# v of three pairs loaded through GpSimd's casting queue, and a new written-out order of work

## The chip, the core and the metric

The kernel runs on one NeuronCore of a Trainium2 chip. The metric is the device time of one execution in microseconds, lower is better. Each kernel is executed several times, and the median is compared. One further execution is recorded by the hardware profiler; all lines of the profile come from that one.

The engines of the core take their instructions from a queue each, in order: TensorE (PE, with its weight loads PEld), VectorE (DVE), ScalarE (ACT), GpSimd (POOL) and SyncE (SP), which here only issues DMAs.

## What is computed

Two stages, one after the other. The first is a gated linear attention over 4 batches, 8 heads, 768 steps and head dimension 48; the second is a two-layer network on the 3072 rows of 384 that the first gives.

```python
def _attn_ref(q, k, v, f_logit):
    f = 1.0 / (1.0 + np.exp(-f_logit))
    state = np.zeros((B, H, D, D))
    for t in range(S):
        state = f[:, :, t, :, None] * state + np.einsum('bhd,bhe->bhde', k[:, :, t], v[:, :, t])
        y[:, :, t] = np.einsum('bhd,bhde->bhe', q[:, :, t], state)

def _moe_ref(x, w_in, w_out):        # x: (3072, 384), w_in: (384, 2048)
    h = x @ w_in
    g = 0.5 * (h + np.sqrt(h * h + 4.0))
    return g @ w_out
```

## The kernel before

The 3072 rows are cut into 12 pairs of 128-step chunks (256 steps, all 8 heads; three pairs make a batch). For each pair `p` the function `describe` makes pieces of work, named by a short code, the pair and a part. Pair 0 is handled in two halves of four heads (`.0` and `.1`) up to its keys and queries; the others in one. The pieces, with the lines that the profile gives for them:

- `lf lq lk lv` (L174): loads of the logits, q, k and v by SyncE, 384 KB each (192 KB for a half of pair 0).
- `ex` (L181), `ut`, `tt`, `ln` (L248), `hi` (L258, or a cast), `lo` (L266): exp of the logits, its sum with one, the product over two steps, its logarithm and the split of that into two fp16 parts. `cu` (L283, L289) sums the logarithms along the steps by matmuls with a triangle; `ep`, `ea` (L312) are exponentials of the sums, from pair 3 on `c1` (L302) adds for the second.
- `qu ku qm km` (L142): q and k scaled by the decays. `tp` and `te` (L390 and a copy) transpose them on TensorE for pairs 0 to 3; `tx` (L373) does it by a DMA for pairs 4 to 11.
- `vc`: v cast to fp16 (L137 on ScalarE, L139 on the others).
- `sc` (L414) scores, `pm` (L429) masks them, `kv` (L442) key times value, `ia` (L452) or `sp` (L468) adds the old state, `sa` and `sb` scale it, `yt` (L492) and `yn` (L501) give y, `yc` copies y out of PSUM. `ge gs gb` are small factors of the state.
- `xp` (L525) and `xe`, or a DMA `xx` (L516) from pair 4 on, transpose y into x.
- `m1` (L541, eight pieces a pair) is x times w_in, `sq` (L550) the square, `rt` (L556) the square root, `gt` (L566) the sum, `m2` (L578, two times four pieces) g times w_out, `ev` copies the result out of PSUM, `st` (L598) stores it.
- `wi0` to `wi3` and `wo0` to `wo3`: the weights, cast to fp16 on the way by DMAs that GpSimd issues (L148, L153), 384 KB of fp16 each. `m1` pieces 0 and 1 need `wi0`, 2 and 3 `wi1`, and so on.

Nothing in the kernel decides the order at run time or at build time: the string `ORDER` names each piece once, with the engine that runs it (after the colon) and the PSUM banks that it fills (after the @). The kernel goes through it word by word, so the order of the words that go to one engine is the order of that engine's queue; the framework only adds the waits. `TABLE:e` and `TABLE:s` load ScalarE's tables for exp and log, and for the square root. `DEPTH` gives how many buffers a tile has, eight PSUM banks are handed out in the words. A piece that needs something late holds up all that stands behind it on its engine. Where a word begins with `wm`, the loop would issue matmuls on constants whose result nobody reads; `ORDER` has no such word.

Of the kernel before, what the change touches and what calls it, by code (L numbers as in the profile page):

```python
# [40 lines left out]
lv2.0:S gt0.0:D yt1:T@23 ku2.0:P sq0.4:A yn1.0:T sa1:D m1.0.3:T@7 rt0.2:A yc1.0:D ia1.1:T m1.0.2:T@4 gt0.1:D sq0.3:A lo3.0:P
yn1.1:T sb1:D xp1.0:T@0 sq0.2:A km2.0:D wo1:P rt0.1:A cu3.0:T@2 lk3.0:S m1.0.6:T@6 qu2.0:P yc1.1:D TABLE:e ln4.0:A c13.0:D
xp1.1:T@3 lq4.0:S qm2.0:P xe1.1:D xe1.0:D m1.0.7:T@3 gt0.5:D ex5.0:A m1.1.1:T@0 gt0.2:D lq3.0:S ea3.0:A vc2.0:P gt0.4:D
tp2.0:T@14 ge3:A sq0.7:A wo0:P ut5.0:D m1.1.3:T@5 sq1.1:A te2.1.0:D tt5.0:P sq0.6:A te2.0.0:D ep3.0:A wo2:P ln5.0:A lk4.0:S
gt0.3:D sc2.0:T@41 TABLE:s rt0.3:A hi4.0:P pm2.01:D kv2:T@27 wo3:P ia2.0:T pm2.00:D m1.1.0:T@1 lo4.0:P sa2:D m1.1.2:T@4
lf6.0:S sq1.3:A gt0.7:D ku3.0:P ia2.1:T sc2.1:T@27 sq1.2:A gt0.6:D m1.1.5:T@3 rt1.1:A pm2.10:D m1.1.4:T@6 hi5.0:P pm2.11:D
sq1.0:A m2.0.00:T@2 km3.0:P gt1.3:D rt1.0:A m2.0.01:T gt1.2:D yt2:T@57 sq1.4:A yn2.0:T gt1.0:D yn2.1:T qu4.0:P sq1.5:A
m1.1.7:T@4 yc2.1:D rt1.2:A m1.1.6:T@1 lo5.0:P gt1.1:D lf7.0:S cu4.0:T@7 qu3.0:D sq1.6:A gs3:P m2.0.10:T@0 sq1.7:A yc2.0:D
qm3.0:P m2.0.11:T rt1.3:A gt1.4:D xp2.0:T@5 m2.0.02:T lk5.0:S gt1.5:D TABLE:e ep4.0:A cu5.0:T@6 gt1.7:D ku4.0:P xp2.1:T@3
m2.0.12:T xe2.0:D lv3.0:S c15.0:D tp3.0:T@45 ex6.0:A c14.0:D m2.0.03:T km4.0:P xe2.1:D ep5.0:A lf8.0:S te3.0.0:D m2.0.13:T  # L50
ge5:A ex7.0:A te3.1.0:D m1.2.2:T@6 ge4:A lv4.0:S ev0.0:A ut7.0:D sc3.1:T@73 sc3.0:T@45 ea5.0:A m2.1.10:T@2 ut6.0:D tt7.0:P
ev0.1:A lq5.0:S gt1.6:D m2.1.11:T ea4.0:A sq2.2:A tt6.0:D m2.1.12:T qm4.0:P vc3.0:A m1.2.0:T@0 pm3.10:D m2.1.13:T ln6.0:A
pm3.00:D sq2.0:A m1.2.3:T@1 pm3.11:D ln7.0:A gb4:P kv3:T@47 tx4.0:S ku5.0:D hi6.0:P sq2.3:A m2.1.00:T@3 TABLE:s rt2.1:A sa3:D
m2.1.01:T st0.01.0:S km5.0:P sp3.1:D tx4.1:S m1.2.1:T@4 pm3.01:D m2.1.02:T ev1.1:D lv5.0:S yt3:T@57 sq2.1:A lo6.0:D qu5.0:P
lq6.0:S yn3.1:T rt2.0:A gt2.3:D m1.2.5:T@2 gt2.2:D m2.1.03:T qm5.0:P yc3.1:A m1.2.4:T@1 gt2.1:D yc3.0:A lk6.0:S ev1.0:A
sc4.1:T@56 gt2.0:D sq2.4:A sc4.0:T@47 m1.2.6:T@3 pm4.11:D sb3:P sq2.5:A lf9.0:S xp3.1:T@0 pm4.00:D rt2.2:A m1.2.7:T@6 vc4.0:P
pm4.01:D m2.2.10:T@4 sq2.7:A st1.01.1:S st0.01.1:S gs4:P gt2.4:D hi7.0:P m2.2.11:T sq2.6:A qu6.0:P gt2.5:D xp3.0:T@7 cu6.0:T@1
rt2.3:A tx5.0:S pm4.10:D m2.2.12:T lo7.0:P TABLE:e ex8.0:A xe3.1:D yt4:T@25 gt2.7:D ku6.0:P yn4.0:T tx5.1:S m2.2.00:T@0
xe3.0:D gt2.6:D kv4:T@67 lq8.0:S c16.0:D ex9.0:A cu7.0:T@3 vc5.0:P sp4.0:D m2.2.01:T ea6.0:A ut8.0:D ep7.0:A m2.2.13:T lk7.0:S
sa4:D tt8.0:P ge6:A yc4.0:A m1.3.0:T@6 c17.0:D ep6.0:A yn4.1:T ev2.1:D m2.2.02:T ea7.0:A gb5:P ut9.0:D gs5:P ln8.0:A  # L60
m1.3.1:T@4 ge7:A yc4.1:D kv5:T@12 sq3.0:A tt9.0:P sp4.1:D sc5.1:T@23 xx4:S sq3.1:A m2.2.03:T pm5.11:D sb4:P ln9.0:A sc5.0:T@57
pm5.10:D TABLE:s rt3.0:A lv8.0:S m1.3.3:T@3 km6.0:P pm5.01:D lq7.0:S m1.3.5:T@2 sp5.0:D m1.3.4:T@7 lv6.0:S ev2.0:D m1.3.2:T@1
sa5:P pm5.00:D sq3.4:A sq3.5:A gt3.1:D yt5:T@05 hi9.0:P st1.01.0:S rt3.2:A yn5.0:T qm6.0:P yn5.1:T m1.4.1:T@4 yc5.0:D sq3.3:A
gt3.5:D m1.3.7:T@0 sq3.2:A gt3.0:D m1.3.6:T@2 lo9.0:P tx6.0:S rt3.1:A gt3.4:D m1.4.3:T@6 vc6.0:P yc5.1:D sq3.7:A m1.4.4:T@7
lv7.0:S gt3.3:D sq3.6:A qu7.0:P m2.3.10:T@5 tx6.1:S rt3.3:A gt3.2:D m1.4.0:T@3 hi8.0:P gs6:D m2.3.11:T lv9.0:S ku7.0:P sq4.1:A
gt3.6:D m2.3.12:T sq4.0:A gt3.7:D kv6:T@12 rt4.0:A lf10.0:S m1.4.2:T@0 sa6:D vc8.0:P sq4.4:A gt4.0:D m2.3.13:T km7.0:P sq4.3:A
m2.3.00:T@1 sp6.1:D xx5:S sq4.2:A gt4.1:D m1.4.6:T@2 rt4.1:A ev3.1:D m1.4.7:T@3 qu8.0:P lk8.0:S sc6.1:T@45 sq4.6:A gt4.3:D
m2.3.01:T gb7:P sq4.7:A pm6.10:D vc7.0:P m1.4.5:T@6 rt4.3:A lf11.0:S pm6.11:D lo8.0:P m2.3.02:T gt4.2:D sq4.5:A sc6.0:T@45
st2.01.0:S st2.01.1:S qm7.0:P m2.3.03:T rt4.2:A gt4.6:D cu8.0:T@0 pm6.00:D TABLE:e ex10.0:A cu9.0:T@2 gt4.7:D m1.5.3:T@4 sb6:P
tx7.0:S gt4.5:D m2.4.10:T@3 ku8.0:P gt4.4:D m2.4.00:T@6 tx7.1:S ge9:A ge8:A ev3.0:D ep9.0:A m2.4.11:T c18.0:D ex11.0:A lq9.0:S  # L70
m2.4.01:T ut10.0:D gs7:P ea8.0:A m2.4.12:T ut11.0:D ep8.0:A lk9.0:S m1.5.2:T@1 sq5.3:A pm6.01:D tt11.0:P m2.4.13:T sq5.2:A
c19.0:D tt10.0:P yt6:T@05 ev4.1:D ea9.0:A lv10.0:S kv7:T@27 yc6.0:D ln11.0:A yn6.1:T gb8:P m2.4.02:T sp7.0:D ln10.0:A TABLE:s
rt5.1:A yc6.1:D sc7.0:T@03 sa7:P m2.4.03:T pm7.00:D xx6:S qm8.0:P m1.5.1:T@2 sp7.1:D m1.5.0:T@0 ev4.0:D st3.01.0:S sq5.1:A
st3.01.1:S gt5.3:D m1.5.4:T@5 st4.01.1:S sq5.0:A qu9.0:P gt5.2:D m1.5.5:T@6 lq11.0:S rt5.0:A sc7.1:T@47 pm7.01:D hi11.0:P
m1.5.7:T@1 sb7:P sq5.5:A gt5.0:D m1.5.6:T@3 sq5.4:A gt5.1:D hi10.0:P m1.6.2:T@0 rt5.2:A pm7.11:D lo11.0:P m2.5.10:T@2 gs8:D
sq5.7:A m2.5.11:T km8.0:P gt5.4:D sq5.6:A m1.6.0:T@7 gt5.5:D rt5.3:A m1.6.3:T@5 pm7.10:D m2.5.12:T gs9:P sq6.2:A tx8.1:S
gt5.6:D ku9.0:P kv8:T@46 sq6.3:A yt7:T@36 sp8.0:D rt6.1:A tx8.0:S yn7.0:T yn7.1:T gt5.7:D m1.6.1:T@4 qm9.0:P sq6.0:A gt6.3:D
m1.6.5:T@1 lk11.0:S sq6.1:A gt6.2:D m2.5.13:T lk10.0:S rt6.0:A yc7.1:D m1.6.4:T@0 km9.0:P ev5.1:A cu11.0:T@5 gt6.1:D sq6.4:A
m2.5.00:T@2 gt6.0:D yc7.0:A sc8.1:T@46 c111.0:D lo10.0:P sq6.5:A xx7:S sc8.0:T@37 m2.5.01:T pm8.11:D rt6.2:A ku11.0:P
m2.5.02:T pm8.10:D tx9.1:S cu10.0:T@6 pm8.00:D m2.5.03:T gt6.4:D TABLE:e ep10.0:A lv11.0:S vc9.0:P m1.6.7:T@3 pm8.01:D  # L80
st4.01.0:S ep11.0:A m1.6.6:T@0 sa8:P gt6.5:D ge11:A ea11.0:A yt8:T@74 c110.0:D sq6.7:A qu11.0:P kv9:T@15 tx9.0:S yn8.0:T
ge10:A ea10.0:A sa9:D yn8.1:T m1.7.6:T@6 sq6.6:A yc8.1:D m1.7.2:T@1 TABLE:s rt6.3:A sp9.1:D lq10.0:S m2.6.00:T@4 vc11.0:P
yc8.0:D gb10:D m1.7.1:T@5 xx8:S ku10.0:P m1.7.3:T@7 sq7.2:A gt6.7:D m2.6.01:T sq7.3:A gt6.6:D m2.6.02:T rt7.1:A ev5.0:D
# [43 lines left out]
def describe(nc, W, ctx_tiles, aps):  # L127
# [28 lines left out]
    for p in range(NP):  # L156
# [9 lines left out]
        for x, (h0, h1) in enumerate(parts):  # L166
            hs = slice(h0, h1)
            nh = h1 - h0
            for s in "fqkv":
                def load(e, bk, s=s, x=x, hs=hs, p=p):  # L170
                    if (s, p) not in T:
                        T[s, p] = sb(s, p, [128, 8, 2, 48], FP32)
# [556 lines left out]
```

## Time and profile before

| | |
|---|---|
| time, median of 11 runs | 197.24 us (193.91 to 199.5) |
| profiled execution | 195.81 us, span 193.6 us |
| TensorE matmul | 171.9 us busy (89%) |
| VectorE, ScalarE, GpSimd | 152.1, 153.5, 117.9 us busy (79%, 79%, 61%) |
| DMA | 32.87 MB, 170 GB/s over the span |
| read, written in HBM | 25.17 MB, 4.72 MB |

The span runs from the first to the last instruction; the time is a little longer. Busy shares are averages over stages: in the first 28 us the matmuls wait for inputs to be prepared, later they follow one another. A line of the timeline gives start and duration in us, engine, line of the kernel, operation, written and read tiles, size, count, and in brackets how long the engine stood idle ahead of it and what it waited for. In the table by stretches each engine has its busy time and in brackets its number of instructions; then come the clock that TensorE was granted (1.00 is full), the mean busy share of the DMA engines, and GB/s.

### The profile page before, as it was taken

How to read it: one execution, taken by the hardware profiler on the slowest of the kernel's cores; microseconds unless marked ns; L12 is line 12 of the kernel's file. 1: busy time of each engine (PE TensorE's matmuls, PEld its weight loads, DVE VectorE, ACT ScalarE, POOL GpSimd, SP SyncE). 2: the span in 40 equal slices, each digit the busy share in tenths (PEclk: the TensorE clock that was granted, in tenths of full speed). 3: DMA queues.
4: the chain of work that ended last, by engine and by line, in shares of the span. 5: the costliest groups of instructions: out<-in, count | busy, mean ns of one | idle time of the engine just before them, and what ended most of it. 6: DMA issues, size and time to landing. Idle time of an engine off the chain costs nothing.

```text
span 193.6 us, 5596 instructions
## 1 busy us (share of the span) xinstructions
PE 171.9 (89%) x2287; PEld 124.3 (64%) x2287; DVE 152.1 (79%) x280; ACT 153.5 (79%) x246; POOL 117.9 (61%) x146
## 2 busy tenths in 40 slices
PE   0348994899999999899999999999989999999990
PEld 0235772667666766687667776877657688767650
DVE  5797898898898999887999988867769787536640
ACT  4685899599989998899979989987756599896600
POOL 5159559898989779939989996859950100000000
PEclk9999999699999999999999999999999999999998
DMA  5999999999987999999999989991687234000623
GB/s 148 271 261 241 249 218 232 253 236 208 261 205 125 217 254 130 272 217 211 212 243 207 244 148 206 187 197 51 54 151 138 43 85 83 3 0 3 163 73 90
DMA packets 80506, 32.87 MB, mean 170 GB/s; under 512 B 73825, under 2 KB 80481, under 8 KB 80481
## 3 DMA queue, kind: packets, MB, share of 16 engines
q1 hardware_dynamic: 76768, 29.37, 74.3%
q0 software_dynamic: 3712, 3.15, 10.1%
q8 instruction: 18, 0.29, 0.6%
q14 instruction: 8, 0.06, 0.1%
HBM read 25.17 MB, written 4.72 MB: 154 GB/s over the span
## 4 chain that ended last, share of the span: by engine, by line
PE 69%; DMA 18%; DVE 4%; issue 2%; POOL 2%; ACT 2%; SPq 1%; DVEq 0%; ACTq 0%
PE ps L578 30%; PE ps L541 27%; DMA xT<-y 6%; DMA win<-in_moe_w_in_dram 4%; DMA f<-in_f_logit_dram 3%; PE ps L414 3%; DMA k<-in_k_dram 2%; DMA qkT<-qk 2%; PE ps L492 2%; PE ps L442 2%; DVE qk L142 2%; PE ps L501 2%; PE ps L283 1%; POOL k L142 1%; PE ps L390 1%
## 5 line engine op out<-in xcount | busy, mean ns | idle before, releaser
L566 DVE SCALAR_TENSOR_TENSOR g<-ps,r 128x512 f16<-128x512 f32 x96 | 62.3, 682 | 17.6 <-ACT r L556 17.6
L541 PE MATMUL ps<-xT,win 128*128 128x256 f16 x576 | 73.6, 275 | 2.1 <-DMA xT<-y 0.8
L578 PE MATMUL ps<-wout,g 128*128 128x384 f16 x384 | 71.1, 326 | 0.0
L550 ACT ACTIVATE hsq<-ps 128x512 f16<-128x512 f32 x96 | 54.0, 592 | 15.7 <-PE ps L541 15.0
L541 PEld LDWEIGHTS <-win 128*128 128x128 f16 x576 | 55.2, 99 | 14.0 <-issue 1.5
L556 ACT ACTIVATE r<-hsq 128x1024 f16<-128x1024 f16 x48 | 50.6, 1057 | 1.2
L578 PEld LDWEIGHTS <-g 128*128 128x128 f16 x384 | 36.1, 98 | 19.5
L429 DVE TENSOR_TENSOR pm<-ps,mask 128x512 f16<-128x512 f32 x48 | 30.8, 681 | 3.0 <-PE ps L414 3.0
L142 POOL TENSOR_TENSOR qk<-q,ea 128x384 f16<-128x384 f32 x22 | 22.2, 1032 | 1.3 <-DVE q L142 0.8
L142 POOL TENSOR_TENSOR k<-k,UT 128x768 f32<-128x768 f32 x9 | 16.3, 1815 | 3.6 <-DMA k<-in_k_dram 1.9
L142 POOL TENSOR_TENSOR qk<-k,ep 128x384 f16<-128x384 f32 x18 | 17.6, 998 | 0.1
L283 PE MATMUL ps<-hl,tri 128*128 128x384 f16 (+1 forms) x34 | 9.3, 376 | 8.8 <-ACT hl L258 6.6
L181 ACT ACTIVATE f<-f 128x768 f32<-128x768 f32 (+1 forms) x13 | 10.3, 791 | 4.7 <-DMA f<-in_f_logit_dram 4.4
L139 POOL CAST v<-v 128x768 f16<-128x768 f32 (+1 forms) x11 | 9.1, 823 | 5.7 <-DMA v<-in_v_dram 5.7
L142 POOL TENSOR_TENSOR UT<-UT 128x384 f32<-128x384 f32 (+1 forms) x9 | 9.1, 1013 | 4.2 <-DVE UT L231 4.2
L142 POOL TENSOR_TENSOR q<-q,UT 128x384 f32<-128x384 f32 x9 | 9.0, 1001 | 3.8 <-DMA q<-in_q_dram 3.8
L266 POOL TENSOR_TENSOR hl<-s,hl 128x384 f16<-128x384 f32 (+1 forms) x11 | 10.4, 950 | 0.8 <-ACT hl L258 0.7
L137 ACT COPY os<-ps 128x384 f32<-128x384 f32 x9 | 4.3, 480 | 8.1 <-PE ps L578 5.0
L414 PE MATMUL ps<-qkT 48*64 48x128 f16 x384 | 9.5, 228 | 1.3 <-ACT qkT L137 0.6
L414 PEld LDWEIGHTS <-qkT 48*64 48x64 f16 x384 | 6.6, 110 | 5.4 <-issue 3.2
L139 DVE CAST y<-ps 128x384 f16<-128x384 f32 x17 | 9.2, 548 | 0.9 <-PE ps L501 0.9
L139 DVE COPY os<-ps 128x384 f32<-128x384 f32 x15 | 8.2, 546 | 2.1 <-PE ps L578 2.1
(71 smaller groups left out, 185.9 us busy)
## 6 DMA issues: line engine op xcount, KB each, us to landing
f<-in_f_logit_dram SPq DMA_DIRECT2D x11, 384.0 KB, 6.0
k<-in_k_dram SPq DMA_DIRECT2D x11, 384.0 KB, 5.6
q<-in_q_dram SPq DMA_DIRECT2D x11, 384.0 KB, 6.2
v<-in_v_dram SPq DMA_DIRECT2D x11, 384.0 KB, 5.8
out_dram<-os SPq DMA_DIRECT2D x22, 192.0 KB, 3.2
win<-in_moe_w_in_dram POOLq DMA_DIRECT2D x4, 384.0 KB, 8.1
wout<-in_moe_w_out_dram POOLq DMA_DIRECT2D x4, 384.0 KB, 8.2
f<-in_f_logit_dram SPq DMA_DIRECT2D x2, 192.0 KB, 3.0
```

Of the source, the lines that this page charges most:

```text
L139: eng(e).tensor_copy(out=o, in_=i)
L142: eng(e).tensor_tensor(out=o, in0=a, in1=b, op=ALU.mult)
L181: nc.scalar.activation(out=t, in_=t, func=AF.Exp, scale=-1.0)
L266: eng(e).tensor_tensor(out=hl[:, 1, hs, 0:D], in0=T["s", p][:, hs], in1=hl[:, 0, hs, 0:D], op=ALU.subtract)
L283: nc.tensor.matmul(out=T["cum", p, m][:, h0 * D:h1 * D], lhsT=tri[:, m], rhs=t[:, hs, 0:D], start=(r == 0), stop=(r == len(terms) - 1), sk ...
L414: nc.tensor.matmul(out=T["sc", p, i, h][64 * cc:64 * cc + 64, j, :], lhsT=t[r, 1, j, i, :], rhs=t[r, 0, j], start=True, stop=True)
L429: eng(e).tensor_tensor(out=T["pm", p, i, h], in0=T["pc", p, i, h] if key in PMACT else T["sc", p, i, h], in1=K["mask"][:, i].unsqueeze(1). ...
L541: nc.tensor.matmul(out=T["h", p, m][:, a], lhsT=K["win"][m // 2][:, j, m % 2 * 256 + a * 128:m % 2 * 256 + a * 128 + 128], rhs=T["xT", p][ ...
L550: nc.scalar.activation(out=T["hsq", p, r][:, a], in_=T["h", p, m].rearrange("p a c t -> p (a c t)"), func=AF.Square, scale=1.0)
L556: nc.scalar.activation(out=T["r16", p, r], in_=T["hsq", p, r], func=AF.Sqrt, scale=0.25, bias=1.0)
L566: nc.vector.scalar_tensor_tensor(out=T["g", p][:, 2 * m:2 * m + 2, :].rearrange("p a t -> p (a t)"), in0=T["h", p, m].rearrange("p a c t - ...
L578: nc.tensor.matmul(out=T["o", p, cc], lhsT=T["g", p][:, jn, cc * 128:(cc + 1) * 128], rhs=K["wout"][jn // 4][:, jn % 4, :], start=(jn == 0 ...
```

## The change

Four things are edited.

1. For pairs 1, 2 and 3 (`VDMA`) there is no load `lv` by SyncE and no cast `vc`. A new piece `vd` on GpSimd loads v straight from HBM into the fp16 tile and casts on the way.
2. `ORDER` is another one throughout: pieces stand elsewhere in the queues, some on another engine, with other PSUM banks. The set of pieces is the same but for `vd`.
3. The stores of the last pair may be issued by ScalarE; the second to last store, `st11.1.0`, is.
4. The branch for `wm` words is gone.

```diff
+VDMA = [1, 2, 3]
...
-            for s in "fqkv":
+            for s in ("fqk" if p in VDMA else "fqkv"):
...
+            if p in VDMA:
+                def vd(e, bk, x=x, hs=hs, p=p):
+                    if ("v16", p) not in T:
+                        T["v16", p] = sb("v16", p, [128, 8, 2, 48], FP16)
+                    bb, t0 = divmod(p * 256, 768)
+                    nc.gpsimd.dma_start(out=T["v16", p][:, hs].rearrange("p h i d -> p h (i d)"),
+                                        in_=v[bb][hs, t0:t0 + 256, :].rearrange("h (p i) d -> p h (i d)", i=2))
...
-                W.add(f"st{p}.{''.join(map(str, cs))}.{i}", "SP" if p in SPLIT_OUT else "S", st, ...
+                W.add(f"st{p}.{''.join(map(str, cs))}.{i}", "SPA" if p in SPLIT_OUT else "S", st, ...
...
-            if name.startswith("wm"):
-                t = ps(banks, [128, 128], FP32)
-                for n in range(int(name[2:])):
-                    nc.tensor.matmul(out=t, lhsT=ident, rhs=ident, start=True, stop=True)
-                continue
```

The queues of GpSimd and TensorE in the first third, by their words (before, then after; ScalarE and VectorE change in the same way):

```
GpSimd before: tt0.1 lo0.1 gs0 lo1.0 wi0 wi2 lo2.0 vc0.0 qm1.0 gb1 wi1 tt3.0 wi3 gs1 vc1.0 tt4.0 gs2 gb2
               hi3.0 ku2.0 lo3.0 wo1 qu2.0 qm2.0 vc2.0 wo0 tt5.0 wo2 hi4.0 wo3 lo4.0 ku3.0
GpSimd after:  lo0.0 qu0.1 lo1.0 wi0 wi2 vd1.0 vc0.1 gs0 qm1.0 wi1 wi3 tt3.0 gb1 tt4.0 hi3.0 lo3.0 gs1 gs2
               gb2 ku2.0 vd2.0 wo0 qu2.0 qm2.0 wo1 wo2 tt5.0 hi4.0 lo4.0 hi5.0 ku3.0
TensorE before: kv0 yt0 yn0.1 ia0.1 xp0.0 xp0.1 tp1.0 m1.0.1 m1.0.0 sc1.0 sc1.1 m1.0.4 m1.0.5 kv1 ia1.0 yt1
               yn1.0 m1.0.3 ia1.1 m1.0.2 yn1.1 xp1.0 cu3.0 m1.0.6 xp1.1 m1.0.7 m1.1.1 tp2.0 m1.1.3 sc2.0 kv2
TensorE after: kv0 yt0 yn0.1 ia0.1 xp0.0 xp0.1 tp1.0 m1.0.0 m1.0.1 sc1.1 sc1.0 m1.0.5 kv1 ia1.0 m1.0.4 yt1
               yn1.0 ia1.1 m1.0.3 yn1.1 m1.0.2 xp1.0 xp1.1 cu3.0 m1.0.6 m1.0.7 tp2.0 m1.1.2 kv2 ia2.0 sc2.0
```

The end of the order, where only the last store differs in kind:

```diff
-m2.11.13:T st11.0.0:S st11.0.1:S ev11.1:A st11.1.0:S st11.1.1:S
+m2.11.13:T st11.0.0:S st11.0.1:S ev11.1:A st11.1.0:A st11.1.1:S
```

## The prediction, made before the changed kernel ran

> **What bounds the kernel now.** I read the shares of the engines first, then the chain of work that ended last, then the timeline and the waits around the one place where that chain leaves TensorE for long.
>
> ```profile
> PE 171.9 (89%) x2287; PEld 124.3 (64%) x2287; DVE 152.1 (79%) x280; ACT 153.5 (79%) x246; POOL 117.9 (61%) x146
> ...
> PE 69%; DMA 18%; DVE 4%; issue 2%; POOL 2%; ACT 2%; SPq 1%; DVEq 0%; ACTq 0%
> ```
>
> TensorE is the bound, but 89% is an average. Priced by the chain (six m1 matmuls 0.655 us, four m2 0.65, a score piece about 0.44, kv 0.46, yt 0.51, and so on), all 162 us of TensorE work comes to 162.65 us; the last matmul ends at 189.2. So 26.55 us are lost in all. I call the loss up to a piece its "slip": its start minus the work ordered ahead of it. m1.0.1 starts at 22.25 with 6.4 ahead: slip 15.85. Further: m1.0.3 16.6 (27.76), m1.0.6 18.3, m1.0.7 20.6, kv2 22.7 (39.97), m2.0.00 23.0 (44.19), tp3 23.2 (51.83), the end 26.55. Thus 6.4 us go between 27.8 and 44.2, and only 3.3 in the 137 us after 51.8. In the timeline that place looks so:
>
> ```profile
> 27.76 0.83 PE L541 MATMUL ps<-xT,win 128*128 128x256 f16 x6 [0.23 <-DMA win<-in_moe_w_in_dram]
> ...
> 30.58 3.05 DVE L142 TENSOR_TENSOR qk<-k,ep 128x384 f16<-128x384 f32 x2 [0.90 <-POOL k L142]
> ...
> 31.47 0.32 PE L283 MATMUL ps<-hl,tri 128*128 128x384 f16 x1 [1.56 <-POOL hl L266]
> ...
> 33.55 0.54 DVE L139 CAST y<-ps 128x384 f16<-128x384 f32 x1
> ...
> 34.15 0.34 PE L525 MATMUL ps<-ident,y 128*128 128x128 f16 x3 [1.51 <-DVE y L139]
> ```
>
> The k load of pair 2, issued at 15.05, landed 13.6 us later (28.65). Only then could GpSimd run ku2.0 (1.81 us); lo3.0 was queued behind it on GpSimd (cu3.0 waits 1.56), and on VectorE yc1.1 behind km2.0 (3.05 for two), which waits for ku2.0: TensorE waits 1.51 more. The idle stretch then costs clock:
>
> ```profile
> 34.00:36.00 2.00, 1.40 (x11) 1.05 (x12) 2.00 (x6) 0.59 (x2) 2.00 (x3) 0.84 1.26 202
> 36.00:38.00 2.00, 2.00 (x38) 1.41 (x36) 1.41 (x3) 1.23 (x3) 1.47 (x3) 0.50 1.19 295
> ```
>
> In this table by stretches the clock follows the five busy columns; the trace has it at half from 35.36 for 3.41 us, so 1.7 us of that loss is clock. Its DMA column stands at 1.19 to 1.26 (packets overlap): until about 60 us inputs arrive as fast as the queues bring them.
>
> **What the Trainium skill says.** "DMA: Bandwidth & Descriptors", section "SWDGE vs HWDGE vs iDMA": a DMA that casts must be GpSimd's, and each DMA engine takes turns between the software and the hardware queues. The trace agrees: in 18 to 20 us it holds 303 software packets (median 96 ns) beside 361 hardware ones (22 to 35 ns), so a win load takes some 2.7 us and leaves the loads of SyncE a quarter of the time. "TensorE: Matmul & The Clock Gate", "Part 1": the clock is halved after an idle window of some 3.4 us that runs freely; the 3.41 us here agree, and where windows fall differs by run. "SBUF — State Buffer", "Who interferes with whom": a VectorE operation with two SBUF inputs contends with GpSimd's reads; km2.0 took 1.25 and 1.88 us here against 0.45 for the median of its kind.
>
> **The change part by part.** The profiled execution took 195.81 us (span 193.6, 2.2 around it); the median of eleven is 197.24, 1.43 higher, and they spread over 5.6 us. I take the difference for further half-clock windows (1.7 us each), which I can't see, and carry it over.
>
> *v of pairs 1 to 3.* Away go three loads of SyncE (their issues took 1.4, 4.4 and 1.4 us), two GpSimd casts of 0.82 (one hidden in GpSimd's waits) and a ScalarE cast of 0.87 at 55.8. Added are three GpSimd DMAs. An issue for 384 or 512 rows takes 0.8; these have 1,024 rows, so 0.8 to 1.6; I take 1.1. On GpSimd that is a wash. The transfer isn't shown: 1,024 packets of 384 bytes read. At the hardware packet's price beside it (690 packets of both kinds in 2 us, half each) 3.0 us; at the software packet's 96 ns, 1,024 x 96 / 16 = 6.1; I take 3.0. Alone it could be the 1.45 at which hardware loads follow one another. The place matters more: GpSimd's queue has wi0, wi2, vd1, wi1, wi3, vd2, wo0, wo1. Software data began at 16.3 before; now lo1.0 waits for hi1.0, moved behind two te copies on ScalarE (12.8 to 13.3), so wi0 is issued at about 14.3 and data begins at 17.0. With 2.7 per weight load and 1.2 to the landing: win0 21.9 (was 21.2), win2 23.6 to 24.6, vd1 27 (v1 was 24.5), win1 29.8 (27.7), win3 32.5 (30.5), vd2 35, wout0 37.6 (44.0 was wout0, 37.4 wout1), wout1 40.2.
>
> *The order, start.* Up to sc0.0 both need the same VectorE rows (0.31 to 0.56 each from k's landing at 7.0); I get sc0.0 at 14.1 against 13.5, yt0 at 19.0 against 19.2, m1.0.0 at 22.0 against 22.25: no gain. kv1 then heads TensorE's queue until vd1 at 27 (25.69 before), and m1.0.4 and yt1 stand behind it. But k2 now lands near 24.4; lo3.0 stands ahead of ku2.0, which runs at 26 instead of 28.7; km2.0 at 29.7 instead of 30.6 and yc1.1 at 30.7 instead of 33.55. So m1.0.3 starts at 29.8 (slip 18.5, worse by 1.9), m1.0.6 at 32.5 (18.8), m1.0.7 at 33.2 (18.9, was 20.6). Then ScalarE: rt0.1 ends at 33.05, table load 1.28, ex5.0 35.2, ut5.0 on VectorE 35.75, two te copies of 0.65 to 37.1, where sc2.0 starts: slip 20.3. gt0.2 and four pm (0.64 each) give banks back up to 41.5, rt0.3 ends at 41.55 as before; m1.1.x and m2.0 run at a slip near 21.9 where it was 23.0. **-1.1**, between -3.5 (if ScalarE isn't the bound there) and +1.
>
> *The order, clock.* The idle stretch of 29.9 to 34.9 becomes four shorter ones (25.3 to 27, 29.3 to 29.8, 35.7 to 37.1, 37.8 to 39). I let six runs in ten be spared the window: 0.6 x 1.7 = **-1.0**, between -1.7 and +1.7.
>
> *The order, steady part.* From 52 us TensorE is dense, so only waits count. An xT transpose needs 0.55 (y copy), its queue and 4.5 to 6.3 to land. Work between the last yn and the first m1 of a pair: pair 4 6.8 before (and it waited 0.77), 5.7 now; pair 6 6.1 before, 5.0 now; pair 8 9.4 and 6.1. Pair 4 may wait 0.8 to 2, pair 6 0.5 to 1. Less the 0.77 of before: **+0.7**, between 0 and +2. The steps moved past SyncE's waits elsewhere keep over 5 us in hand. ev copies have a median of 1.5 us to free a bank where they had 3.1; a copy is 0.55, so I charge nothing; if a gt of 0.68 stands ahead, each such case costs some 0.2.
>
> *Last store.* The tail is:
>
> ```profile
> 189.23 0.48 ACT os L137
> ```
>
> SyncE issued the two last stores at 189.74 and 190.33, 2.2 us each to landing. ScalarE now issues one right after its copy, so both go at 189.75: **-0.6**; at worst 0, if ScalarE's issue takes as much longer. Nothing is queued behind it. The zero matmuls: ORDER held none, so 0.
>
> Sum: 197.24 - 1.1 - 1.0 + 0.7 - 0.6 = **195.2**. On the profiled execution the same gives about 193.8.
>
> **The rivals.** *Same time (0.23):* weights arrive 2 us later, and the half-clock window falls into another gap. For it: SyncE's loads sat up to 14.7 us in the queues, the DMA columns are above 1. Against it: win1 is needed only after 27, and the six us were lost to ku2.0. Start and clock then give 0: 197.24 + 0.7 - 0.6 = 197.3.
>
> *Slower (0.22):* the casting transfer costs the software price. vd1 stands ahead of win1 and win3, and kv1 blocks TensorE's queue. With 6.1 in place of 3.0, vd1 lands at 30 and win1 at 33: start -1.1 + 3.1 = +2.0, and idle of over 4 us brings the clock window back and half of another, +0.9: 197.24 + 2.0 + 0.9 + 0.7 - 0.6 = 200.2. Gain in the start turns to loss when a v transfer takes over 4.1 us (3.0 + 1.1), some 64 ns a packet.
>
> *Better (0.13):* ScalarE is not in the way at 33 to 41, the start gives 3.5: 192.8.
>
> **How the numbers follow.** Forecast 0.42 at 195.2, own range 194 to 196.5, half of it below 195.27. A run-to-run spread like this tells about 1% from no change. Faster by over 1% (under 195.27): half of 0.42, all of 0.13, and 0.06 from the near side of "same": 0.40. Slower by over 1% (over 199.2): 0.20 from the casting case's 0.22. The rest, 0.40. The range reaches from 192.8 to 199.6: it leaves out half of the best case (0.07) and half of the slow one (0.11).
>
> **What would show it.** Right: lo3.0 done before ku2.0, TensorE's wait for hl gone, m1.0.7 near 33, v landing within 11 us of its issue at GpSimd (queue included), one store issued by ScalarE, the clock at full from 22 to 185. Wrong: TensorE waiting at kv for v16 beyond 28, m1.0.3 after 31, waits for xT over 2 us in all, GpSimd's DMA issue for v over 2 us. My walk through the start uses nominal rows; one contended VectorE operation of 1.9 us in place of 0.45 would already move it by half of what I forecast.

## The result, and the profile after

The changed kernel takes 198.63 us, median of 12 runs (197.15 to 201.63); the kernel before 197.24 beside it, median of 47. The ratio is 1.0163, interval 1.0124 to 1.0201: slower by 1.6%, where 195.2 us and a gain of 1% were forecast. The time lies inside the range of 192.8 to 199.6; the case that was to end slower (a casting transfer at 96 ns a packet) is not what happened. A ratio is taken over the runs within 1.5% of the fastest of the same kernel, a median over all runs; so the two can differ.

The profiled execution of the changed kernel took 197.15 us (193.8 was forecast for it), with a span of 195.3; that of the kernel before 195.81 and 193.6. From the page of the changed kernel, the busy time of the engines and the chain of work that ended last, by engine:

```profile
PE 169.5 (87%) x2287; PEld 123.7 (63%) x2287; DVE 151.3 (77%) x278; ACT 154.0 (79%) x248; POOL 115.7 (59%) x146
...
PE 70%; DMA 16%; ACT 4%; SPq 3%; DVE 2%; POOL 1%; issue 1%; DVEq 0%
```

TensorE is busy 2.4 us less (171.9 before), and yet the span is 1.7 longer. The clock explains most of the first: no half-clock window fell into this execution (mean granted clock 0.997, 0.988 before), and the old order without such a window has 170.5 us (b3, below). By slips, as the prediction defined them, the picture is this; the last column but one is that profile of the old order, and the last is experiment a1, whose words are those of the changed kernel but for one store late in the order. Its only half-clock window comes at 103.8 us, so its start can be read without one. The last piece's slip is taken at its start, where the prediction's 26.55 is taken at its end:

| | before | after | old order without a half-clock window (b3) | new start once more (a1) |
|---|---|---|---|---|
| start of m1.0.0 | 22.90 | 22.83 | 23.01 | 21.18 |
| start of m1.0.3 | 27.76 | 31.14 | 27.85 | 29.84 |
| start of m1.0.7 | 34.94 | 35.11 | 33.32 | 33.46 |
| slip at tp3 (some 51 us) | 23.25 | 22.70 | 22.01 | 21.41 |
| slip of the last piece | 26.38 | 26.40 | 25.90 | 27.28 |
| last matmul ends | 189.19 | 189.22 | 188.71 | 190.09 |
| from there to the end of the span, the "tail" | 4.40 | 6.05 | 4.05 | 4.29 |

So three things stand out: the last matmul ends where it did although the clock was better; the start has not clearly won (the same words gave a slip of 22.70 in one profile and 21.41 in another, on both sides of the old order's 22.01); and the tail is 1.65 us longer. What sets two profiles of one start apart is open; TensorE begins at half clock and gets the full one at 18.4 us in a1, 19.9 after, 21.0 in b3 and 21.7 before, which may be part of it. First the start. The changed file has more lines, so the lines of the pieces are shifted: m1 is L550 in it, kv L451, m2 L587. From the timeline of the changed kernel, TensorE alone (start us, us, engine, line, operation, tiles, count, idle before it and what ended that):

```profile
25.74 0.49 PE L550 MATMUL ps<-xT,win 128*128 128x256 f16 x3
28.53 0.51 PE L451 MATMUL ps<-v,qk 64*128 64x96 f16 x16 [2.29 <-DMA v<-in_v_dram]
...
31.14 0.83 PE L550 MATMUL ps<-xT,win 128*128 128x256 f16 x6 [0.23 <-DMA win<-in_moe_w_in_dram]
...
33.60 0.34 PE L534 MATMUL ps<-ident,y 128*128 128x128 f16 x3 [0.64 <-DVE y L139]
33.87 0.50 PE L283 MATMUL ps<-hl,tri 128*128 128x384 f16 x2
34.20 0.34 PE L289 MATMUL ps<-ind,hl 128*128 128x3 f16 x8
34.46 1.47 PE L550 MATMUL ps<-xT,win 128*128 128x256 f16 x12
```

L451 at 28.53 is kv1: TensorE waits 2.29 us for v of pair 1. L550 at 31.14 is m1.0.3, which waits for win1. What the new order was to remove is removed: TensorE's 1.56 for hl and its 1.51 for y, shown before, have become nothing and 0.64 (xp1.1, at 33.60). The old order can lose them too: in b3, where k of pair 2 landed at 27.46 instead of 28.67, TensorE waits 0.28 for hl and not for y.

The stretches of the changed kernel that answer the two shown of before (busy time and number of instructions of TensorE, its weight loads, VectorE, ScalarE and GpSimd; then granted clock, DMA share, GB/s):

```profile
34.00:36.00 2.00, 2.00 (x23) 1.52 (x22) 2.00 (x5) 1.97 (x3) 1.43 (x2) 1.00 1.40 196
36.00:38.00 2.00, 1.45 (x38) 1.10 (x37) 2.00 (x5) 2.00 (x6) 0.59 (x1) 1.00 1.27 213
```

The clock stayed at 1.00 here. Of the eight profiles below that have this start with the casting load, only this one and a1 were spared a window there. Now the tail, from the timeline of the changed kernel:

```profile
187.95 0.56 DVE L139 COPY os<-ps 128x384 f32<-128x384 f32 x1 [1.06 <-PE ps L587]
187.99 0.86 ACT L137 COPY os<-ps 128x384 f32<-128x384 f32 x2 [2.41 <-DMA out_dram<-os]
189.25 0.48 ACT L137 COPY os<-ps 128x384 f32<-128x384 f32 x1 [0.40 <-PE ps L587]
189.76 0.54 ACTq L607 DMA_DIRECT2D out_dram<-os  x1
```

The last line is the edited store, now issued by ScalarE at 189.76, within 0.01 of the forecast. But the second line is new: ScalarE's two copies of pair 10 (ev10.1, ev10.0) waited 2.41 us for a store that still read the buffer that they overwrite. In the new `ORDER` that store, st8.01.1, stands in SyncE's queue behind both stores of pair 9, which wait for ev9.1. SyncE issued st8.01.0 at 172.25, st8.01.1 only at 183.96, and it landed 4.0 us after that, at 187.92. All stores behind it are then late: pair 10's go at 188.88 and 189.51 (186.06 and 186.71 before), SyncE's last at 191.77 (190.35 before).

### The profile page after: what moved, and what is told of

Same layout as the page of the kernel before. It is cut to its first block, busy times and chain, and to the rows that moved or that the text cites. A ratio compares the mean times of both kernels' runs of the same rounds, so it can differ in the third digit from the quotient of the medians.

```text
span 195.3 us, 5587 instructions
## 1 busy us (share of the span) xinstructions
PE 169.5 (87%) x2287; PEld 123.7 (63%) x2287; DVE 151.3 (77%) x278; ACT 154.0 (79%) x248; POOL 115.7 (59%) x146
## 4 chain that ended last, share of the span: by engine, by line
PE 70%; DMA 16%; ACT 4%; SPq 3%; DVE 2%; POOL 1%; issue 1%; DVEq 0%
PE ps L587 29%; PE ps L550 27%; DMA qkT<-qk 6%; DMA win<-in_moe_w_in_dram 6%; PE ps L423 3%; SPq L174 3%; DMA f<-in_f_logit_dram 3%; PE ps L501 2%; PE ps L283 2%; PE ps L451 2%; DMA out_dram<-os 2%; PE ps L510 2%; POOL qk L142 1%; DVE qkT L139 1%; ACT hsq L559 1%
## 5 line engine op out<-in xcount | busy, mean ns | idle before, releaser
L550 PE MATMUL ps<-xT,win 128*128 128x256 f16 x576 | 71.7, 273 | 2.1 <-DMA win<-in_moe_w_in_dram 1.2
L587 PE MATMUL ps<-wout,g 128*128 128x384 f16 x384 | 70.7, 326 | 0.0
L550 PEld LDWEIGHTS <-win 128*128 128x128 f16 x576 | 54.8, 98 | 12.2 <-DMA win<-in_moe_w_in_dram 2.2
L587 PEld LDWEIGHTS <-g 128*128 128x128 f16 x384 | 36.1, 98 | 20.0
L142 POOL TENSOR_TENSOR k<-k,UT 128x768 f32<-128x768 f32 x8 | 14.5, 1812 | 3.5 <-DMA k<-in_k_dram 3.5
L266 POOL TENSOR_TENSOR hl<-s,hl 128x384 f16<-128x384 f32 (+1 forms) x11 | 9.7, 881 | 6.9 <-ACT hl L137 4.2
L139 DVE COPY os<-ps 128x384 f32<-128x384 f32 x16 | 8.8, 550 | 4.4 <-PE ps L587 2.9
L142 POOL TENSOR_TENSOR q<-q,UT 128x384 f32<-128x384 f32 (+1 forms) x9 | 8.7, 970 | 4.7 <-DMA q<-in_q_dram 4.7
L142 POOL TENSOR_TENSOR UT<-UT 128x384 f32<-128x384 f32 x8 | 8.3, 1043 | 3.0 <-DVE UT L231 3.0
L139 POOL CAST v<-v 128x768 f16<-128x768 f32 (+1 forms) x9 | 7.1, 789 | 4.4 <-DMA v<-in_v_dram 4.4
L231 DVE TENSOR_SCALAR UT<-f 128x768 f32<-128x768 f32 (+1 forms) x13 | 8.9, 703 | 0.5 <-ACT f L181 0.5
L248 ACT ACTIVATE s<-UT 128x384 f32<-128x384 f32 (+1 forms) x13 | 6.5, 499 | 3.2 <-DVE UT L142 1.8
```

What stands on the lines that cost most here:

```text
L139: eng(e).tensor_copy(out=o, in_=i)
L142: eng(e).tensor_tensor(out=o, in0=a, in1=b, op=ALU.mult)
L266: eng(e).tensor_tensor(out=hl[:, 1, hs, 0:D], in0=T["s", p][:, hs], in1=hl[:, 0, hs, 0:D], op=ALU.subtract)
L550: nc.tensor.matmul(out=T["h", p, m][:, a], lhsT=K["win"][m // 2][:, j, m % 2 * 256 + a * 128:m % 2 * 256 + a * 128 + 128], rhs=T["xT", p][ ...
L587: nc.tensor.matmul(out=T["o", p, cc], lhsT=T["g", p][:, jn, cc * 128:(cc + 1) * 128], rhs=K["wout"][jn // 4][:, jn % 4, :], start=(jn == 0 ...
```

## The experiments

Each kernel below is the changed or the former kernel with a few words of `ORDER` moved. The table gives what was timed; "ratio" is against the kernel before on the same chip.

| kernel | median us (runs) | ratio, 95% interval | tail in the profile | slip at tp3, of the last piece |
|---|---|---|---|---|
| before | 197.24 (47) | | 4.40 | 23.25, 26.38 |
| after | 198.63 (12) | 1.0163, 1.0124 to 1.0201 | 6.05 | 22.70, 26.40 |
| a1_tail | 197.77 (4) | 1.0143, 1.0046 to 1.0241 | 4.29 | 21.41, 27.28 |
| a2_tail_sp | 195.68 (4) | 1.0039, 0.9951 to 1.0126 | 4.57 | 23.19, 27.41 |
| a3_v1 | 198.62 (4) | 1.0175, 1.0089 to 1.0260 | 6.02 | 24.86, 28.67 |
| a5_vall | 198.61 (4) | 1.0197, 1.0126 to 1.0268 | 5.92 | 24.76, 27.53 |
| a4_tx | 196.30 (14) | 1.0062, 1.0019 to 1.0104 | 6.31 | 23.12, 25.77 |
| b1_order | 196.97 (20) | 1.0074, 1.0032 to 1.0115 | 4.38 | 22.73, 25.77 |
| b2_vd | 197.99 (20) | 1.0113, 1.0071 to 1.0155 | 5.00 | 25.06, 28.76 |
| b3_act | 194.99 (4) | 0.9885, 0.9822 to 0.9948 | 4.05 | 22.01, 25.90 |

A slip holds 1.7 us for each half-clock window ahead of it: a2, a3, a5 and b2 have two in their profile, before, a1 (at 103.8) and a4 one, after, b1 and b3 none. With four runs, a median can stand 1 us off by the clock alone. One order's slip differs between profiles as well: from tp3 to the end the old order gains 3.13 (before), 3.89 (b3) and 3.04 (b1). In b2 the last store lands 3.35 us after the last matmul, as in the kernel before; the rest of its tail of 5.00 comes behind that.

### The tail

a1_tail moves one store of the changed kernel; a2_tail_sp also gives the last store back to SyncE; b3_act gives it to ScalarE in the old order, alone.

```diff
 a1:  -st9.01.0:S ... st9.01.1:S ... st8.01.1:S        (all of the changed kernel)
      +st8.01.0:S st8.01.1:S ... st9.01.0:S ... st9.01.1:S
 a2:  as a1, and st11.1.0:A -> st11.1.0:S
 b3:  the kernel before, with st11.1.0:S -> st11.1.0:A
```

> The changed kernel with one store, st8.01.1, moved ahead in SyncE's queue, from behind the stores of pair 9 to right behind st8.01.0. Theory (order of the stores): in the changed kernel ev10.0 and ev10.1 wait on ScalarE until 187.99 us for st8.01.1 to land, the stores of pair 10 go at 188.9 in place of 186, and the last store of SyncE goes at 191.8. Moved, SyncE's last store goes at about 189.8 and ScalarE's, landing 3.1 to 3.4 us after 189.8, ends the kernel: 1.0 us less than the changed kernel. Rival (the store on ScalarE is itself what lengthens the tail): its landing stays the last thing and the time falls by less than 0.3.

> As the one before, and st11.1.0 is SyncE's again. If a store by ScalarE lands as slowly as in the changed kernel's profile (3.4 us against 2.2 for SyncE's in the kernel before), SyncE's two at 189.75 and 190.35 land at 192.55, before ScalarE's at 193.1: another 0.6 less. If the forecast was right that ScalarE's store is worth 0.6, this is 0.6 more than the one before.

> The kernel before with the second to last store issued by ScalarE, nothing else. Forecast: the tail behind the last matmul is 4.40 in the kernel before; with both stores issued at 189.75 it falls by 0.6. From the profiles of the changed order, where ScalarE's store took 3.4 us to land: 0.3 or nothing. Rival (a third DMA queue lengthens the end of the kernel): 0.3 or more slower.

From the timeline of a1_tail, the copies of the last pairs:

```profile
186.36 0.84 ACT L137 COPY os<-ps 128x384 f32<-128x384 f32 x2
188.83 0.56 DVE L139 COPY os<-ps 128x384 f32<-128x384 f32 x1 [1.05 <-PE ps L587]
190.13 0.48 ACT L137 COPY os<-ps 128x384 f32<-128x384 f32 x1 [2.93 <-PE ps L587]
```

ScalarE's wait for out_dram is gone, its copies run 3.8 us ahead of the last one instead of 1.3, and the tail falls from 6.05 to 4.29: the queued store is the cause of the longer tail. The store by ScalarE gives 0.28 of that (4.57 with SyncE) and 0.35 in the old order (4.05 against 4.40), not 0.6. It is not that ScalarE's store lands late: it took 2.24 us from issue to landing in b3 and 2.36 in a1, against 2.19 for SyncE's last one in the kernel before. But with both stores issued at the same moment, SyncE's took 2.47 and 2.51, and it ended last. The 3.42 us of ScalarE's store in the changed kernel, from which the expectations above start, belong to its crowded end: four stores of SyncE were issued from 0.9 us before it to 1.1 us after it, and one of them took 3.14. The timed gain of b3 (1.1%) is larger than a tail of 0.35 can make. Three of its four runs had the clock near full, and the mean of such runs of the kernel before is 194.7, that of these three 194.8: nothing timed speaks for more than the profile shows. In a1's timed runs the tail's gain does not stand out (ratio 1.0143), and a2, which should have been 0.3 us slower than a1, came out 2.1 faster: four runs each are too few for tenths.

### The transposed loads behind stores

The changed kernel has two more waits in the steady part. From its timeline (TensorE, two places):

```profile
67.07 0.64 PE L423 MATMUL ps<-qkT 48*64 48x128 f16 x32 [0.96 <-DMA qkT<-qk]
...
103.09 0.41 PE L423 MATMUL ps<-qkT 48*64 48x128 f16 x15 [1.75 <-DMA qkT<-qk]
```

tx4.0 stands behind a store and lq6.0, and its partner tx4.1 went 3.2 us before it (58.14 and 61.38); tx7.1 stands behind two stores of pair 3 (issued 97.34, landed 5.7 later). a4_tx moves both next to their partners.

```diff
-tx4.1:S ... st0.01.0:S ... lq6.0:S ... tx4.0:S        +tx4.1:S tx4.0:S ... st0.01.0:S ... lq6.0:S
-tx7.0:S ... st3.01.0:S ... st3.01.1:S ... tx7.1:S     +tx7.0:S tx7.1:S ... st3.01.0:S ... st3.01.1:S
```

> The changed kernel with two DMA transposes moved ahead in SyncE's queue: tx4.0 right behind tx4.1 (from behind a store and a load of q), tx7.1 right behind tx7.0 (from behind two stores of pair 3). Theory (the new order of SyncE's queue brings qkT late): TensorE's waits for qkT, 1.0 us ahead of sc4 and 1.75 in sc7, fall under 0.5 in all, the slip at the end and the time by about 2 us. Rival (xT or another step comes next): the waits for qkT go, the time falls by less than 0.7.

From the timeline of a4_tx, the same matmuls:

```profile
66.95 0.64 PE L423 MATMUL ps<-qkT 48*64 48x128 f16 x32
...
102.55 0.42 PE L423 MATMUL ps<-qkT 48*64 48x128 f16 x16
```

Both waits, 2.7 us, are gone. A wait of 1.23 us for xT of pair 4 comes up in their place (at 85.0), and the slip gained after tp3 falls from 3.70 to 2.65 only; one order's profiles differ by nearly as much (above). The time falls from 198.63 to 196.30, with 14 runs, and the intervals of the two ratios lie apart: two words moved in SyncE's queue are worth 1% in this order. The profile shows 1.05 of the 2.3 us; the rest stays open.

### The casting loads of v

a3_v1 and a5_vall put v back to SyncE in the new order, for pair 1 and for all three. b2_vd makes the opposite: the kernel before with the three casting loads alone.

```diff
 a3:  -vd1.0:P (behind wi2)   +lv1.0:S behind lf4.0, +vc1.0:P behind tt4.0
 a5:  as a3; +lv2.0:S behind lf5.0, +vc2.0:P behind qm2.0; +lv3.0:S behind lf7.0, +vc3.0:P ahead of tt7.0
 b2:  the kernel before without lv1-3, vc1-3; +vd1.0:P behind wi2, +vd2.0:P behind lo3.0, +vd3.0:P ahead of tt7.0
```

> The changed kernel with v of pair 1 loaded by SyncE again (right behind f of pair 4) and cast by GpSimd (behind tt4.0); pairs 2 and 3 stay with the casting queue. Theory (v in the software queue holds up kv1 and the weights behind it): kv1 starts near 25.7 in place of 28.5, m1.0.3 near 29 in place of 31.1, m1.0.6 near 32; TensorE's slip at tp2.0 falls by 1 to 2 us and so does the time. Rival (the weights are late because lo1.0 and so wi0 are issued later, and the queues are full anyway): win1 lands within 0.7 us of where it did, the time within 0.5.

> The changed kernel with v of pairs 1, 2 and 3 all loaded by SyncE and cast by GpSimd; the order is otherwise the changed one. Theory: 1 to 2 us less than the changed kernel, most of it from pair 1, since kv2 waited only 0.3 us there and not for v. Rival (the order alone costs all): no change beyond 0.5 us, or worse, since GpSimd has the three casts of 0.82 us back.

> The kernel before with the casting loads alone: v of pairs 1 to 3 by GpSimd (vd1 behind wi2, vd2 behind lo3.0, vd3 ahead of tt7.0), the order as it was, the last store by SyncE. Theory from the runs that put v back: the casting load delays the weights (kv1 by 1 to 3 us, win1 by 2) but frees k of pair 2 by some 4 us, and so the start is no worse: time within 1 us of the kernel before. Rival (the forecast's slow case, that the casting load holds up weights and TensorE): 2 to 4 us slower.

From the timeline of b2_vd (TensorE; kv1, then m1.0.3):

```profile
27.98 0.51 PE L451 MATMUL ps<-v,qk 64*128 64x96 f16 x16 [1.44 <-DMA v<-in_v_dram]
...
31.01 1.46 PE L550 MATMUL ps<-xT,win 128*128 128x256 f16 x6 [1.47 <-DMA win<-in_moe_w_in_dram]
```

The wait for v and the late win1 come with the casting load, in the old order too (there win1 landed at 30.96 instead of 27.71), and the kernel is 1.1% slower. In the new order taking it away gives nothing. From the timeline of a3_v1:

```profile
28.86 0.82 PE L550 MATMUL ps<-xT,win 128*128 128x256 f16 x6
...
34.44 0.50 PE L534 MATMUL ps<-ident,y 128*128 128x128 f16 x3 [3.77 <-DVE y L139]
...
35.63 1.66 PE L550 MATMUL ps<-xT,win 128*128 128x256 f16 x7
```

m1.0.3 starts 2.3 us sooner than after (28.86), but then TensorE stands 3.77 us for y, and m1.0.6 starts at 35.63 instead of 34.46. The yc1.1 that it waits for stands behind km2.0, as in the old order, and k of pair 2 came late: it landed at 23.20 in the changed kernel, at 30.18 in a3 and at 29.46 in a5. In a3 GpSimd's ku2.0 waits 1.86 us for it, and km2.0 2.38 us for ku2.0. So where the casting load is gone the weights are sooner and the k behind v in SyncE's queue is later.

How long a casting load takes the trace of the changed kernel shows in its packets. From the table of DMA queues for the stretch 24 to 26 us (packets, MB, share of 16 engines):

```profile
q0 software_dynamic: 650, 0.13, 72.8%
q1 hardware_dynamic: 649, 0.24, 71.3%
```

The two kinds take turns one to one, as the prediction held after the Trainium skill's page "DMA: Bandwidth & Descriptors", section "SWDGE vs HWDGE vs iDMA". The packets of v write 192 bytes each, at a median of 35 ns: not the 96 of a weight packet. At this rate 1,024 of them take 3.2 us. They are mixed with 296 weight packets at both ends, so v's stretch is 22.93 to 28.10, 5.2 us; what v adds to the queue is less: vd1 landed 3.1 us after win2 (28.48 and 25.36), and 3.1 again in a1 (26.83 and 23.70), 3.0 in b2.

### The start's order alone

b1_order makes, in the kernel before, the two moves by which the prediction explained the 6.4 us lost between 27.8 and 44.2: lo3.0 ahead of ku2.0 on GpSimd, yc1.1 ahead of km2.0 on VectorE. The second puts both of them ahead of sb1 as well, which its expectation does not say.

```diff
-ku2.0:P ... lo3.0:P      +lo3.0:P ku2.0:P
-sb1:D ... km2.0:D ... yc1.1:D      +yc1.1:D km2.0:D sb1:D
```

> The kernel before with two moves: lo3.0 ahead of ku2.0 on GpSimd, and yc1.1 ahead of km2.0 on VectorE. It tests the reading that the 6.4 us lost between 27.8 and 44.2 come from what stands behind ku2.0 and km2.0. Theory: TensorE's waits of 1.56 and 1.51 us go, m1.0.7 starts near 32 in place of 34.9, there is no half-clock window at 35, and the time falls by 2 to 3 us. Rival (the next late thing, the table loads and ex5.0 on ScalarE or wout, takes over): slip at tp3 no lower than 22.5 and less than 1 us won.

From the timeline of b1_order, TensorE:

```profile
29.95 0.49 PE L282 MATMUL ps<-hl,tri 128*128 128x384 f16 x2
30.27 0.34 PE L288 MATMUL ps<-ind,hl 128*128 128x3 f16 x8
32.53 0.82 PE L540 MATMUL ps<-xT,win 128*128 128x256 f16 x6 [1.92 <-DVE sn L141]
33.19 0.33 PE L524 MATMUL ps<-ident,y 128*128 128x128 f16 x3
33.97 1.47 PE L540 MATMUL ps<-xT,win 128*128 128x256 f16 x12 [0.45 <-DVE xT L138]
```

Both waits are gone (cu3 runs at 29.95 instead of 31.47), and nothing is won: m1.0.6 waits 1.92 at 32.53, m1.0.7 starts at 33.97 where the old order at full clock has 33.32, and the slip at tp3 is 22.73 against 22.01. By the ratio it is 0.7% slower; its median equals that of the kernel before on its chip (196.97 and 196.89).

Two things hold m1.0.6 here. The sn that the line names is sb1, which frees its PSUM bank and in b1 came to stand behind km2.0. And its weights, win3, landed only at 31.71. So without the displaced sb1 it could have started at most 0.8 us sooner. In b3 the weights alone hold it:

```profile
31.87 0.83 PE L550 MATMUL ps<-xT,win 128*128 128x256 f16 x6 [1.10 <-DMA win<-in_moe_w_in_dram]
```

From m1.0.3 to m2.0.00 the slip grows by 5.1 us in b3 and 5.5 in b1, where the kernel before lost 6.4 with 1.7 of half clock in it. So the waits for hl and y that the prediction read were not what bounded that place. Next in line is win3; what follows it was not taken apart.

### Old and new order with plain copies for transposing DMAs

To try both repairs of SyncE's queue together, eight more kernels leave out the transposition of pairs 4 to 11: their `tx` and `xx` are plain DMA copies of as many bytes in the same places of the order (and the exponents of these pairs are scaled by 0.01 to keep numbers finite). q0 and r0 have the old order, q1 the new one, q2 and r1 the new one with both repairs, r3 with that of the tail alone, r2 both repairs and v by SyncE as in a5, and q3 the old order with vd1 alone. The q and the r kernels each shared a chip.

> Base of four kernels that leave out the transposition of pairs 4 to 11: their transposing DMAs are plain copies of the same bytes (and the exponents of these pairs are scaled by 0.01 to keep the numbers finite). The order is that of the kernel before. If a transposing DMA costs no more than its landing, which TensorE hardly waits for in the old order, this base is within 1% of the kernel before; start and tail as there: m1.0.3 near 27.8, m1.0.7 near 33 to 35, tail near 4.4 us.

> The new order with the same copies in place of the transposing DMAs. My theory (queue of SyncE at the end, and the start): plain copies land sooner, so the 2.8 us of waits for qkT go; what is left against the base is the tail (+1.6) and the start (0 to +1): slower than the base by 1.5 to 2.5 us, tail near 6. Rival (the queued transpositions were all of the loss): within 0.5 us of the base.

> q1 with both repairs of SyncE's queue together: st8.01.1 right behind st8.01.0, and tx4.0, tx7.1 each behind its partner. My theory: tail 6 to 4.3, so faster than q1 by 1.5 us or more, and within 1 us of the base. Rival (the new order is slower in its middle, or at half clock, whatever SyncE does): tail repaired, but the last matmul ends as much later, as in the single repair, and the time stays that of q1.

> The base with the casting load of pair 1 alone (vd1 behind wi2 on GpSimd), the rest of the order as before. Theory that vd1 ahead of win1 and win3 costs the start: kv1 near 28, m1.0.3 near 31 (3 later than the base), half-clock window beginning at that wait, time 1 to 2 us above the base. Rival (the loads of pairs 2 and 3 made the loss of the kernel with all three): kv1 below 26.5, time within 0.7 us of the base.

> The base again (old order, plain copies in place of the transposing DMAs of pairs 4 to 11, exponents of these pairs scaled by 0.01), so that the three others have it on the same chip: 194.4 us.

> New order with copies and both repairs of SyncE's queue (st8.01.1 behind st8.01.0; tx4.0, tx7.1 behind their partners). If SyncE's queue was what made the new order slower: 192 us, under the base by 1 to 2.5 us. Rival (the gain of the first look was the chip's clock in four runs): at the base, within 0.7 us.

> As the repaired new order, but v of pairs 1 to 3 by SyncE and casts (lv1 behind lf4.0, lv2 behind lf5.0, lv3 behind lf7.0; casts on GpSimd). If the casting loads cost in themselves, kv1 comes 2 us earlier and this one is 1 us faster than the repaired order. Rival (with SyncE free of three loads k of pair 2 comes sooner, which is worth as much): within 0.7 us of it, or slower.

> New order with copies and the repair of the tail alone. If tail and queued transfers add up: 1.3 us above the kernel with both repairs (the slip that the unrepaired one gained after tp3), tail near 4.3, m1.6.2 and m2.9.00 at a slip some 1.3 above tp3's. Rival (copies land soon enough, the tail was all): equal to it within 0.5 us.

| kernel | median us (runs) | ratio to the kernel before | tail | slip at tp3, of the last piece |
|---|---|---|---|---|
| q0, old order | 194.37 (4) | 0.9886, 0.9813 to 0.9958 | 4.38 | 21.66, 22.29 |
| r0, the same | 194.25 (21) | 0.9852, 0.9810 to 0.9893 | 4.38 | 24.85, 25.48 |
| q1, new order | 195.92 (4) | none given | 6.09 | 23.48, 24.76 |
| q2, both repairs | 191.54 (4) | 0.9867, 0.9779 to 0.9955 | 4.27 | 22.53, 22.47 |
| r1, the same | 192.48 (9) | 0.9878, 0.9827 to 0.9929 | 4.25 | 23.35, 23.53 |
| r3, tail repaired | 192.45 (6) | 0.9896, 0.9853 to 0.9940 | 4.27 | 23.37, 24.75 |
| r2, repairs, v by SyncE | 193.81 (22) | 0.9918, 0.9881 to 0.9955 | 4.05 | 23.74, 24.13 |
| q3, old order and vd1 | 194.42 (12) | 0.9979, 0.9940 to 1.0017 | 4.44 | 26.88, 27.51 |

r0 has two half-clock windows in its profile, q0 none and the others one each. From the timeline of q1, ScalarE's copies ahead of the last stores:

```profile
186.39 0.86 ACT L137 COPY os<-ps 128x384 f32<-128x384 f32 x2 [2.45 <-DMA out_dram<-os]
187.61 0.48 ACT L137 COPY os<-ps 128x384 f32<-128x384 f32 x1 [0.36 <-PE ps L587]
```

From the timeline of q2, the same copies:

```profile
181.55 0.84 ACT L137 COPY os<-ps 128x384 f32<-128x384 f32 x2
185.32 0.48 ACT L137 COPY os<-ps 128x384 f32<-128x384 f32 x1 [2.93 <-PE ps L587]
```

Nearly the same wait as in the changed kernel, 2.45 us, and the same tail, 6.1; the moved store takes both away here too. q1's median is 1.6 us above the old order's, about what its tail is longer (1.7); with the repairs the median is 1.8 to 2.8 us below the old order's. By the ratios the repaired order (0.987 and 0.988) and the old one (0.989 and 0.985) are level. Of the runs with a mean clock of 0.995 or more, q2 and r1 have one each, both 191.0, and q0 two with a mean of 192.3, r0 seven with 191.7. So once SyncE's queue is repaired the new order is not slower; that it is faster, by some 1 us, one run each does not show. r3 is as fast as r1, though its steady part loses 1.4 us of slip (from the timeline a wait of 0.95 for qkT at 102.18 is a part) and r1's 0.2: within these few runs the second repair does not show in the time, other than with transposing DMAs. r2 is not faster than r1 but 1.3 us slower, the intervals overlapping: in the new order no cost of the casting loads shows against loads of v by SyncE. q3 repeats b2's finding: kv1 at 27.81, m1.0.3 at 31.49 (27.94 in q0) and a ratio 0.9% above q0's, though the medians are equal. At a clock of 0.995 or more its five runs average 194.1, 1.9 us above q0's two. So a cost of the casting load shows in the old order and not in the new one.

## Why the prediction was wrong, step by step

**What bounds the kernel.** Right as to TensorE and its 162.65 us of work. Wrong as to the 6.4 us between 27.8 and 44.2: they were put down to ku2.0 and km2.0, the releasers that the lines name. b1 takes these waits away and wins nothing, and in b3 they are all but absent and 5.1 us are lost all the same: win3, which m1.0.6 needs, lands at 30.5 to 31.8 in the three profiles of the old order.

**The order, start: -1.1 forecast, between -0.6 and +0.7 measured** (slips at tp3 of 21.41 in a1 and 22.70 after, against 22.01 in b3, none with a half-clock window ahead). The term that failed is the base: the slip of 23.0 already held the half-clock window, 1.2 us of it by the profiles of before and b3 (23.25 and 22.01 at tp3), and the step "clock" counted six tenths of 1.7 once more. Against the old order at full clock, 22.01, the forecast slip of 21.9 was no gain at all.

The walk itself held. In a1 it is right to within 0.5 us from v on: vd1 landed at 26.83 (27 forecast), win1 at 29.80 (29.8), win3 at 32.43 (32.5); m1.0.3 started at 29.84 (29.8), m1.0.6 at 32.81 (32.5), m1.0.7 at 33.46 (33.2). The profile of the changed kernel runs later, and two of the signs of being wrong came true in it, kv1 beyond 28 (28.53, after 2.29 of waiting) and m1.0.3 after 31 (31.14). There win0 and win2 were already 0.8 to 0.9 us behind the forecast, vd1 1.5 (28.48), and m1.0.6 and m1.0.7 2.0 and 1.9; over the eight profiles of this start kv1 begins at 26.8 to 28.5. That a1 meets the forecast so closely is in part luck. The price of 3.0 us for v was right by what it added to the queue, 3.1. Its working was not as written: 690 packets of both kinds in 2 us, half each, would give 5.9; 690 in 1 us give 3.0, and 1,299 in 2 us were measured. The 96 ns on which the slower rival stood did not occur; its place, kv1 behind vd1, was right, at 35 ns a packet.

**The order, clock: -1.0 forecast.** The profiled execution had no window, yet over all runs the changed kernel has a mean granted clock of 0.984 (12 runs), the kernel before 0.990 (118 runs). A difference of 0.006 in 195 us is about 1.2 us more, not less, and the 30 runs of a1 to a5 have 0.984 too, on two chips where the kernel before has 0.993 (7 runs) and 0.990 (51). The forecast shortened the idle stretch at 30 to 35 and gave the new gap, which it had at 25.3 to 27, no window: that term failed. In the profile TensorE works 0.23 us of the stretch 26 to 28, where it had 1.67 before. In seven profiles of kernels with vd1 (a4, b2, q1, q2, r1, r3, q3) a window begins between 27.2 and 31.2, at the waits for v and win1 or just behind them; a2's begins at 25.9, a1's at 103.8. Of the eight with the new start two were spared, not six in ten. "TensorE: Matmul & The Clock Gate", section "Part 1", says that the window runs freely and what it hits varies by run; the traces agree, with lengths of 3.41 us or twice that.

**The order, steady part: +0.7 forecast.** From tp3 to the end the slip grows by 3.70; 3.13 in the profile of before and 3.89 in b3. The sum came near, the mechanism was another: xT of pairs 4 and 6, for which it was charged, was not what TensorE waited for, but qkT of pairs 4 and 7, by transfers moved behind stores in SyncE's queue; the xT wait of pair 4 shows only once these are gone (1.23 us in a4). The sentence "the steps moved past SyncE's waits elsewhere keep over 5 us in hand" is the step that failed: these two did not, and cost 2.7 us of waits. Without their waits (a4) the time is 2.3 us lower.

**Last store: -0.6 forecast, +1.65 measured in the tail.** The issue time was right to 0.01 us. The gain of the store itself is 0.3, since SyncE's store, issued together with ScalarE's, takes 0.3 us longer to land than alone (b3). That term was mis-sized; the one that failed is not in the sum: of the moved stores only the last two were followed. st8.01.1 was moved behind the stores of pair 9, and the `os` buffer that it holds delays ScalarE's copies of pair 10 by 2.41 us. "ev copies: I charge nothing" looked at how long they take to free a bank, not at what they wait for.

**In sum**, forecast -2.0, measured +1.4 in the medians. By the profiles without a half-clock window, after against b3: start +0.7, steady part -0.2, tail +2.0 (b3 has ScalarE's store as well), together the 2.5 by which their spans differ (195.3 and 192.8). The means of the runs near full clock are 197.4 (after, 2 runs) and 194.7 (before, 51). Firm in this is the tail: 5.9 to 6.3 in all five profiles that have st8.01.1 behind pair 9, 4.0 to 4.6 in all six profiles of the new order that do not. Start and steady part differ between profiles of one order by about as much as between the orders. Tail and queued transfers are both shown, in the profiles, by a repair that takes the wait away; in the timed runs the second shows (a4) and the first does not with four runs (a1). Not measured are the changed kernel with both repairs and transposing DMAs kept, so whether it would beat the kernel before stays open, and the casting loads of pairs 2 and 3 alone.

## What to carry to other kernels

When an order is changed, walk each in-order queue that issues DMAs to its very end, and for each moved store ask who next writes its buffer: here a store behind another engine's late copy stopped the copies of the pair after that. Take the half-clock time out of a base before a gain is measured from it, and out of both sides. Look at two profiles of the same stretch before a difference of 1 us is explained: a1 and the changed kernel have one start, and its slip differs by 1.3. A wait that the profile names is only worth its length if what stands next in line is not as late; test it by removing it alone.

## What the runs showed of the hardware

- A store of 96 KB by SyncE landed 2.2 us after its issue when it was issued alone (the last of the kernel before). Issued at the same moment as one by ScalarE, it took 2.47 to 2.51 and ScalarE's 2.24 to 2.36 (b3, a1, q2, r1, r2, r3).
- A casting load of 192 bytes written per packet had a median of 35 ns a packet, where casting weight loads have 96; beside loads by SyncE it moved one packet for each of theirs. 1,024 packets pushed the next landing of the software queue back by 3.1 us (after, a1). Its issue on GpSimd took 0.91 to 0.97 us.
- Runs of one kernel spread by 2% with the granted clock: those of the kernel before, on four chips, average 194.7 us where its mean is 0.995 or more (51 runs), and 198.5 where it is 0.981 to 0.985 (22 runs).
- Plain DMA copies in place of the transposing ones make the old order 1.1 to 1.5% faster (q0, r0), more than was expected. From tp3 on its slip grows by 0.63 us in both, where the old order with transposing DMAs gains 3.0 to 3.9; TensorE has no wait over 0.15 us there, against 1.6 us (before) to 2.4 us (b3) for xT, for ScalarE's copies of results and for qkT.
